# Residue outside, quarter and feature inside: another order of the first transform's data in an FFT and max-out kernel

## The chip, the cores and the metric

The kernel runs on one core of a Trainium2 chip. The metric is the device time of one execution in microseconds (us). Three runs of the kernel before the change took 436.28, 437.46 and 439.57 us: median 437.46. One further execution was profiled. Durations below are from that one.

Engines are named as the profile names them: PE is the matrix engine (TensorE), PEld its weight loads, DVE VectorE, ACT ScalarE, POOL GpSimd, SP the engine that issues most DMAs. PSUM is the memory that PE writes; SBUF holds everything else on the chip.

## The reference

A two-dimensional Fourier transform of eight batches of 3072 x 256 numbers, of which the real part is kept, and then a feed-forward layer whose hidden values are the greatest of three products:

```python
def _attn_ref(x):                       # x: (8, 3072, 256) float32
    X = np.fft.fft(x, axis=1)
    X = np.fft.fft(X, axis=2)
    return X.real.astype(np.float32)

def _moe_ref(x, w1, w2, w3, w_out):     # x: (24576, 256); w1..w3: (256, 768); w_out: (768, 256)
    h = np.maximum(np.maximum(x @ w1, x @ w2), x @ w3)
    return (h @ w_out).astype(np.float32)
```

## The kernel before, in words

The transform over 3072 rows is done as 24 x 128. **Stage one** (method `s` of class `Mix`, line 331 for the matmuls) transforms over 24 rows. Its input x0 has 96 partitions: four feature quarters g of 24 rows each; the 256 features are 4 quarters of 64 features dl. For each dl one matmul takes x0[:, dl, :] (96 x 128) as its weights and streams the 96 columns of a constant block, `m24blk`, that holds the same 24 x 24 table once for each quarter. The result is 128 x 96: 128 row positions by (quarter g, residue r), r being the 24 outputs of the short transform (13 cosines, 11 sines). Five (once four) dl share one PSUM tile, each with 96 columns side by side. `DLS` lists the 13 groups in the order in which they are done, from the middle of dl outward. ACT copies each group to `ub` in SBUF as bf16 (line 333; for batch 0 DVE takes two of them).

**The folds** (method `fold`, lines 337 to 354) use that the second transform, over the 256 features, takes features d and 256 - d together: E is their sum, O their difference. DVE computes both from `ub`, dl against 64 - dl and quarter g against 3 - g, into `zE` and `zO`, which are laid out as (dl, g, r) with r innermost: 24 residues for E and 26 for O. `fold(k, which)` does k = 0, 1, 2 from the middle outward; k = 2 also does the features 0, 64 and 128 in small instructions of their own. The instructions read and write runs of 24 residues.

**Stage two** (method `k`, lines 369 to 378, and `end`, 387 to 389) transforms over the 128 row positions. For each residue r its weights are zE[:, :, r] or zO[:, :, r], 128 partitions by 128 features. As r is innermost in zE and zO, these weights have a step of 24 or 26 elements. They multiply columns of cosine and sine tables, 128 columns for the residues 1 to 11 and 64 for 0 and 12, and one column in `end`: 53 matmuls a batch in six groups. ACT copies the results to `tE` and `tO`.

**The layer** takes tE and tO as the moving operand of further matmuls. The second transform is folded into the weights: `gE`, `gO` and `gD` are products of w2 - w1, w3 - w1 and the transform's table, `gw` is the table's product with w1 and w_out. A batch is 3 blocks of 512 row positions by 6 slices of the hidden width (18 units). In each unit `unit_plus` (lines 398, 399), `unit_minus` (406), the maxima of ACT and DVE (412, 413) and ten matmuls with w_out from a queue (422) are issued; DVE adds the linear part (451), and the result goes out by POOL's indirect DMA (456) and SP's (466). The PSUM tiles of `unit_plus`, `pse2` and `pse3`, have two buffers each.

The order of the instructions on each engine is written out by hand. While batch b goes through its 18 units, the tables `ahead0` (b = 0) and `ahead` (later batches) place the pieces of batch b + 1 behind the layer's work of single units, from unit 9, 6 or 5 on: two or three groups of stage one a unit (`s0` to `s12`), the folds (`fA0` to `fC1`, letters for k and digits for E or O), then the groups of stage two (`kE0` to `kO2`, `end`). POOL turns the input of a batch in four casts (line 118), which wait for the last fold of the batch before. For batch 0 stage one, the folds and the first groups of stage two run at the start, before any unit; there x0 keeps dl innermost, so that its weights have a step of 64 elements, while the x0 of later batches has them side by side.

Other names that the change touches: `dvec` (line 150) holds the feature numbers for the tables of the second transform, in the order of zE's 128 columns. POOL zeroes the entries of `zO` that no fold writes (lines 179, 180).

Of the kernel before, what the change touches and what calls it, by code (L numbers as in the profile page):

```python
# [10 lines left out]
BF16 = mybir.dt.bfloat16  # L11
INT32 = mybir.dt.int32
AX = mybir.ActivationFunctionType
ALU = mybir.AluOpType
# [19 lines left out]
def kernel(  # L34
# [9 lines left out]
    nc = tc.nc  # L44
# [17 lines left out]
    consts = ctx.enter_context(tc.tile_pool(name="consts", bufs=1))  # L62
# [4 lines left out]
    z_pool = ctx.enter_context(tc.tile_pool(name="zbuf", bufs=1))  # L67
    t_pool = ctx.enter_context(tc.tile_pool(name="tbuf", bufs=2))

    m24blk = consts.tile([96, 96], BF16, tag="m24blk")  # L70
# [4 lines left out]
    cos_t = consts.tile([128, 13 * 128], BF16, tag="cos_t")  # L75
    sin_t = consts.tile([128, 13 * 128], BF16, tag="sin_t")
    nsin_t = consts.tile([128, 13 * 128], BF16, tag="nsin_t")
# [11 lines left out]
    sgn = consts.tile([128, 1], FP32, tag="sgn")  # L89
    dif = consts.tile([128, 1], FP32, tag="dif")  # L90
    t_mid = consts.tile([128, 2, B], BF16, tag="t_mid")
    zO = consts.tile([128, 128 * 26], BF16, tag="zO")

    def x_rows(b):
        return x[b].rearrange("(a bb) (g dl) -> g a bb dl", bb=128, g=4)
# [32 lines left out]
    def iota(t, pattern, base=0, cm=0):  # L128
        nc.gpsimd.iota(t, pattern, base=base, channel_multiplier=cm,
                       allow_small_or_imprecise_dtypes=True)  # L130
# [17 lines left out]
    j128 = gen.tile([128, 128], FP32, tag="j128")  # L148
    iota(j128, [[24, 128]])
    dvec = gen.tile([128, 128], FP32, tag="dvec")  # L150
    for g in range(2):
        iota(dvec.rearrange("p (dl g) -> p g dl", g=2)[:, g, :], [[1, 64]], base=64 * g)

    x0_first = x0_pool.tile([96, 128 * 64], BF16, name="x0", tag="x0")
    x0v = x0_first.rearrange("p (bb dl) -> p bb dl", dl=64)
# [4 lines left out]
    for jh in range(2):  # L160
        for wsrc, wdst in ((moe_w1, w1_bf), (moe_w2, w2_bf), (moe_w3, w3_bf)):
            wld = nc.gpsimd.dma_start(
                out=wdst.rearrange("p (fc j) -> p fc j", fc=2)[:, :, jh * 384:(jh + 1) * 384],
                in_=wsrc.rearrange("(fc p) j -> p fc j", fc=2)[:, :, jh * 384:(jh + 1) * 384])
            if jh == 0 and wdst is w2_bf:
                first_half = wld
    nc.gpsimd.dma_start(out=wout_bf.rearrange("p (jc c) -> p jc c", jc=NJC),
                        in_=moe_w_out.rearrange("(jc p) c -> p jc c", jc=NJC))
# [7 lines left out]
    nc.gpsimd.tensor_scalar(out=rows_v[:, :, 11], in0=rows_v[:, :, 11], scalar1=late,  # L176
                            scalar2=None, op0=ALU.add)
    nc.gpsimd.tensor_copy(rows_m, rows_f)
    nc.gpsimd.memset(zO.rearrange("p (c r) -> p c r", r=26)[:, :, 24:26], 0.0)
    nc.gpsimd.memset(zO[:, 0:26], 0.0)  # L180

    consts_of = {}
    for (name, value) in (("half_pi", 0.5 * math.pi), ("rnd", ROUND), ("n24", -24.0),
                          ("n256", -256.0), ("n3072", -3072.0)):
        c = gen.tile([128, 1], FP32, name=name, tag=name)
# [21 lines left out]
    pi13 = gen.tile([128, 13], FP32, tag="pi13")  # L207
    nc.vector.tensor_scalar(out=pi13, in0=i13, scalar1=pidx, scalar2=None, op0=ALU.mult)
    nc.vector.tensor_tensor(
        out=m24blk.rearrange("p (g r) -> p g r", g=4),  # L210
        in0=t24.unsqueeze(1).to_broadcast([96, 4, 24]),
        in1=ind24.unsqueeze(2).to_broadcast([96, 4, 24]), op=ALU.mult)

# [2 lines left out]
    q = gen.tile([128, 13 * 128], FP32, tag="q")  # L216
    turn = float(2.0 * math.pi / 3072.0)
    for (r0, r1) in ((0, 7), (7, 13)):
        cs = slice(r0 * 128, r1 * 128)
        n = r1 - r0  # L220
        nc.vector.scalar_tensor_tensor(
            out=v[:, cs].rearrange("p (r j) -> p r j", j=128),
            in0=j128.unsqueeze(1).to_broadcast([128, n, 128]), scalar=pidx,
            in1=pi13[:, r0:r1].unsqueeze(2).to_broadcast([128, n, 128]),
# [14 lines left out]
    for fc in range(2):  # L239
# [3 lines left out]
            out=vm[:, fc * 256:(fc + 1) * 256].rearrange("p (k c) -> p k c", c=128),  # L243
            in0=dvec.unsqueeze(1).to_broadcast([128, 2, 128]), scalar=pf[:, fc:fc + 1],
            in1=half.rearrange("p (k c) -> p k c", c=128), op0=ALU.mult, op1=ALU.add)
# [15 lines left out]
    def product(i, half, jh, pool, tag):  # L261

        psg = pool.tile([128, 512], FP32, name="psg", tag=tag)
        hs = slice(half * 128, (half + 1) * 128)
        for k, (table, wt) in enumerate(((md, (w2_bf, w3_bf)[i]), (nmd, w1_bf))):
            for fc in range(2):
                nc.tensor.matmul(  # L267
                    psg[:, 0:384], table[fc][:, hs],
                    wt[:, fc * DFF + jh * 384: fc * DFF + jh * 384 + 384],
                    start=(k == 0 and fc == 0), stop=(k == 1 and fc == 1))  # L270
        return psg
# [43 lines left out]
    class Mix:  # L315

        def __init__(self, b):
            self.b = b
            self.ub = u_pool.tile([128, 64 * 96], BF16, name="ub", tag="ub")
            self.zE = z_pool.tile([128, 128 * 24], BF16, name="zE", tag="zE")  # L320
            self.tE = t_pool.tile([128, NHALF], BF16, name="tE", tag="tE")
            self.tO = t_pool.tile([128, NHALF], BF16, name="tO", tag="tO")
            self.u = self.ub.rearrange("p (dl g r) -> p dl g r", g=4, r=24)
            self.e = self.zE.rearrange("p (dl g r) -> p dl g r", g=2, r=24)
            self.o = zO.rearrange("p (dl g r) -> p dl g r", g=2, r=26)

        def s(self, k, x0, pool=ps_f, evict=nc.scalar.copy):
            (d0, d1) = DLS[k]
            ps1 = pool.tile([128, 512], FP32, name="ps1", tag="ps")
            for i in range(d1 - d0):  # L330
                nc.tensor.matmul(ps1[:, i * 96:(i + 1) * 96], x0[:, d0 + i, :], m24blk,  # L331
                                 start=True, stop=True)
            evict(out=self.ub[:, d0 * 96:d1 * 96], in_=ps1[:, 0:(d1 - d0) * 96])  # L333

        def fold(self, k, which):

            u, e, o = self.u, self.e, self.o
            dst, op = ((e, ALU.add), (o, ALU.subtract))[which]
            for (lo, hi) in (((20, 45),), ((10, 20), (45, 55)), ((1, 10), (55, 64)))[k]:
                for g in range(2):  # L340
                    nc.vector.tensor_tensor(
                        out=dst[:, lo:hi, g, 0:24], in0=u[:, lo:hi, g, :],
                        in1=u[:, 64 - lo:64 - hi:-1, 3 - g, :], op=op)
            if k < 2:
                return
            nc.vector.tensor_tensor(out=dst[:, 0, 1, 0:24], in0=u[:, 0, 1, :],
                                    in1=u[:, 0, 3, :], op=op)
            if which == 0:
                nc.vector.tensor_copy(e[:, 0, 0, :], u[:, 0, 0, :])
            else:  # L350
                nc.vector.tensor_scalar(out=o[:, 0, 0, 1:12], in0=u[:, 0, 2, 13:24],
                                        scalar1=-1.0, scalar2=None, op0=ALU.mult)
                nc.vector.tensor_copy(o[:, 0, 0, 13:24], u[:, 0, 2, 1:12])
                self.folded = nc.vector.tensor_copy(o[:, 0, 0, 24:26], u[:, 0, 2, 0:13:12])

        def k(self, which, g):

            er = self.zE.rearrange("p (c r) -> p c r", r=24)
            orr = zO.rearrange("p (c r) -> p c r", r=26)
            parts = [(r, r * 128, 128) for r in range(4 * g + 1, min(4 * g + 5, 12))]  # L360
            if g == 2:
                parts += [(0, 0, 64), (12, 12 * 128, 64)]
            ps2 = ps_f.tile([128, 512], FP32, name="ps2", tag="ps")
            c0 = 0
            for (r, k0, wd) in parts:
                outsl = ps2[:, c0:c0 + wd]
                if which == 0:
                    two = 1 <= r <= 11
                    nc.tensor.matmul(outsl, er[:, :, r], cos_t[:, k0:k0 + wd],  # L369
                                     start=True, stop=not two)  # L370
                    if two:
                        nc.tensor.matmul(outsl, er[:, :, 12 + r], sin_t[:, k0:k0 + wd],  # L372
                                         start=False, stop=True)
                else:
                    io = 24 if r == 0 else 25 if r == 12 else 12 + r
                    nc.tensor.matmul(outsl, orr[:, :, r], nsin_t[:, k0:k0 + wd],  # L376
                                     start=True, stop=False)
                    nc.tensor.matmul(outsl, orr[:, :, io], cos_t[:, k0:k0 + wd],  # L378
                                     start=False, stop=True)
                c0 += wd  # L380
            nc.scalar.copy(out=(self.tE, self.tO)[which][:, g * 512:(g + 1) * 512], in_=ps2)  # L381

        def end(self):
            er = self.zE.rearrange("p (c r) -> p c r", r=24)
            orr = zO.rearrange("p (c r) -> p c r", r=26)
            ps3 = ps_f.tile([128, 512], FP32, name="ps3", tag="ps")
            nc.tensor.matmul(ps3[:, 0:1], er[:, :, 0], cos_t[:, 64:65], start=True, stop=True)
            nc.tensor.matmul(ps3[:, 1:2], orr[:, :, 0], nsin_t[:, 64:65], start=True, stop=False)
            nc.tensor.matmul(ps3[:, 1:2], orr[:, :, 24], cos_t[:, 64:65], start=False, stop=True)
            nc.scalar.copy(out=t_mid[:, :, self.b], in_=ps3[:, 0:2])  # L390

    def unit_plus(te, to, jc, n):
# [159 lines left out]
    for k in range(13):  # L552
        m.s(k, x0f, pool=ps_s,
            evict=nc.vector.tensor_copy if k in (1, 3) else nc.scalar.copy)
# [160 lines left out]
```

## Time and profile before

| | |
|---|---|
| median of three runs | 437.46 us |
| the profiled execution | 437.27 us, of which its span 435.5 us |
| first stage-one matmul | 21.0 us after the span's start |
| TensorE's granted clock | 1.00 of full speed |
| stage one, L331 | 512 matmuls of 96 columns, 211 ns from start to end each |
| stage two, L369, L372, L376, L378, L387 to L389 | 424 matmuls of 128, 64 or 1 columns |
| folds, L341 | 160 DVE instructions on 600, 240 or 216 elements, 473, 279 and 271 ns each for O |
| evictions of stage one by ACT, L333 | 102, 556 ns each |

Times in the profile are from the start of the span. A line of instructions in order of time has the start, the time from there to the end of the last of the group, the engine, the line of the kernel, the operation with its tiles (output <- inputs), the shape and how many. In brackets stands how long the engine was idle before, and what ended that. A line of a table of groups has, behind the count, the busy time in us and the mean duration of one in ns, and then the idle time before them. PE's matmuls overlap one another: one starts while those before it still drain.

### The profile page before, as it was taken

Reading aid. Unit: us, or ns where it says so; the run is one execution under the profiler, and the core shown is the slowest. Engines: PE = TensorE matmul, PEld = TensorE weight load, DVE = VectorE, ACT = ScalarE, POOL = GpSimd, SP = SyncE. Lnnn points to the kernel's source line nnn. Section 1 sums busy time; section 2 is a strip of 40 time slices with the busy share of each in tenths; the row PEclk is TensorE's granted clock in tenths of the full one; section 3 lists DMA queues with packets and bytes.
Section 4 is the critical chain, followed back from the end, with each engine's and each line's share of the span. In section 5 each row is a group of like instructions: output and inputs, shape, how many; then the busy total and the mean of one; then the engine's idle time right before and its main releaser. Section 6 shows DMA issues by size and latency. Waiting matters only on the chain.

```text
span 435.5 us, 9209 instructions
## 1 busy us (share of the span) xinstructions
PE 413.3 (95%) x3252; PEld 277.8 (64%) x3252; DVE 309.6 (71%) x643; ACT 274.2 (63%) x512; POOL 237.8 (55%) x256
## 2 busy tenths in 40 slices
PE   0499999999999999999999999999999999999996
PEld 0275666666676667666676667666676666665665
DVE  7766668765975688666976679666976679567673
ACT  3576668667755776657765676657765676654550
POOL 7646661796269714974279514974279612214320
PEclk9999999999999999999999999999999999999999
DMA  9999999379712968169822968159822222111313
GB/s 118 121 160 129 135 169 177 103 146 169 181 53 69 162 139 189 64 115 168 165 87 76 176 123 198 61 114 165 167 92 74 73 62 75 61 50 55 105 62 132
DMA packets 127333, 51.58 MB, mean 118 GB/s; under 512 B 109233, under 2 KB 124344, under 8 KB 127288
## 3 DMA queue, kind: packets, MB, share of 16 engines
q1 hardware_dynamic: 104936, 35.80, 44.1%
q0 software_dynamic: 20624, 14.68, 17.2%
q10 hardware_dynamic: 1728, 0.52, 0.7%
q8 instruction: 25, 0.41, 0.4%
q14 instruction: 20, 0.16, 0.2%
HBM read 28.31 MB, written 25.17 MB: 123 GB/s over the span
## 4 chain that ended last, share of the span: by engine, by line
PE 90%; DVE 3%; ACT 2%; DMA 1%; POOL 1%; SPq 1%; ACTq 0%; issue 0%; POOLq 0%
PE po L422 28%; PE pse L398 14%; PE pse L406 14%; PE pse L399 14%; PE ps L331 6%; PE po L446 4%; PE pl L438 2%; PE ps L378 1%; DMA xs<-in_x_dram 1%; PE ps L369 1%; PE ps L376 1%; PE ps L372 1%; PE warm L548 1%; POOL x L118 1%; PE psg L267 1%; SPq L100 1%
## 5 line engine op out<-in xcount | busy, mean ns | idle before, releaser
L412 ACT ACTIVATE stmp<-pse 128x512 bf16<-128x512 f32 x288 | 167.8, 604 | 57.5 <-PE pse L399 52.3
L456 POOL DMA_INDIRECT out_dram<-ot,rows_m x92 | 100.2, 1089 | 166.2 <-DVE ot L451 156.2
L413 DVE TENSOR_TENSOR hp<-pse,stmp 128x512 bf16<-128x512 f32 x144 | 99.5, 691 | 100.6 <-ACT stmp L412 61.4
L118 POOL CAST x<-xs 96x2048 bf16<-96x2048 f32 x28 | 106.2, 3801 | 10.3 <-DMA xs<-in_x_dram 7.9
L398 PE MATMUL pse<-tE,gE 128*128 128x512 bf16 x288 | 109.2, 379 | 0.4
L399 PE MATMUL pse<-tO,gO 128*128 128x512 bf16 x288 | 109.0, 379 | 0.0
L413 DVE TENSOR_TENSOR hm<-pse,stmp 128x512 bf16<-128x512 f32 x144 | 98.8, 686 | 7.6 <-ACT stmp L412 7.3
L422 PE MATMUL po<-wout_bf,hp 128*128 128x256 bf16 x576 | 86.1, 273 | 0.0
L406 PE MATMUL pse<-tO,gD 128*128 128x512 bf16 x288 | 85.6, 379 | 0.0
L422 PE MATMUL po<-wout_bf,hm 128*128 128x256 bf16 x576 | 78.6, 273 | 0.0
L333 ACT CAST ub<-ps 128x480 bf16<-128x480 f32 (+1 forms) x102 | 51.7, 556 | 35.0 <-PE ps L331 35.0
L422 PEld LDWEIGHTS <-hp 128*128 128x128 bf16 x576 | 56.4, 98 | 26.1
L422 PEld LDWEIGHTS <-hm 128*128 128x128 bf16 x576 | 56.3, 98 | 16.3
L451 DVE TENSOR_TENSOR ot<-po,even 128x512 f32<-128x512 f32 x92 | 62.8, 683 | 0.0
L406 PEld LDWEIGHTS <-gD 128*128 128x128 bf16 x288 | 27.9, 98 | 32.1
L398 PEld LDWEIGHTS <-gE 128*128 128x128 bf16 x288 | 28.6, 99 | 19.5 <-issue 0.8
L399 PEld LDWEIGHTS <-gO 128*128 128x128 bf16 x288 | 28.2, 98 | 19.9 <-issue 1.6
L446 PE MATMUL po<-gw,tO 128*128 128x512 bf16 x92 | 34.9, 379 | 0.0
L331 PE MATMUL ps<-m24blk,x 96*128 96x96 bf16 x512 | 33.3, 211 | 0.9 <-POOL x L118 0.5
L331 PEld LDWEIGHTS <-x 96*128 96x128 bf16 x512 | 30.5, 111 | 3.0 <-POOL x L118 0.7
L381 ACT CAST tO<-ps 128x512 bf16<-128x512 f32 x24 | 14.0, 585 | 24.8 <-PE ps L378 24.8
L442 ACT COPY even<-pl 128x512 f32<-128x512 f32 x46 | 27.3, 594 | 0.3
(123 smaller groups left out, 335.9 us busy)
## 6 DMA issues: line engine op xcount, KB each, us to landing
xs<-in_x_dram SPq DMA_DIRECT2D x112, 192.0 KB
out_dram<-ot SPq DMA_DIRECT2D x90, 128.0 KB
out_dram<-ot,rows_m POOLq DMA_INDIRECT x92, 3.9
w_bf<-in_moe_w_dram POOLq DMA_DIRECT2D x6, 192.0 KB, 5.9
out_dram<-ot SPq DMA_DIRECT2D x17, 64.0 KB
xs<-in_x_dram SPq DMA_DIRECT2D x8, 96.0 KB
x<-in_x_dram POOLq DMA_DIRECT2D x8, 96.0 KB, 11.3
xs<-in_x_dram ACTq DMA_DIRECT2D x4, 96.0 KB
```

The costliest lines, as they stand in the source:

```text
L118: cast = nc.gpsimd.tensor_copy(turned[b][:, :, ch * 32:(ch + 1) * 32], raw.pop((b, ch)).rearrange("p (bb dl) -> p dl bb", dl=64))
L331: nc.tensor.matmul(ps1[:, i * 96:(i + 1) * 96], x0[:, d0 + i, :], m24blk, start=True, stop=True)
L333: evict(out=self.ub[:, d0 * 96:d1 * 96], in_=ps1[:, 0:(d1 - d0) * 96])
L398: nc.tensor.matmul(pse[:, 0:n], gE[i][:, js], te, start=True, stop=False)
L399: nc.tensor.matmul(pse[:, 0:n], gO[i][:, js], to, start=False, stop=True)
L406: nc.tensor.matmul(pse, gD[i][:, js], to, start=False, stop=True, skip_group_check=True)
L412: nc.scalar.activation(out=stmp[:, 0:n], in_=pses[0][:, 0:n], func=AX.Relu)
L413: nc.vector.tensor_tensor(out=dst, in0=src3, in1=stmp[:, 0:n], op=ALU.max)
L422: nc.tensor.matmul(po, hcols(jc), wout_bf[:, jc * 256:(jc + 1) * 256], start=False, stop=(jc == NJC - 1), skip_group_check=True)
L446: nc.tensor.matmul(po, to[:, cp], gw[:, 256:768], start=True, stop=True)
L451: nc.vector.tensor_tensor(out=ot.rearrange("p (h c) -> p h c", h=2), in0=po.rearrange("p (h c) -> p h c", h=2), in1=lin.unsqueeze(1).to_br ...
L456: stored(nc.gpsimd.indirect_dma_start(out, bass.IndirectOffsetOnAxis(ap=rows_m[0:128 - lo, b * 12 + slot: b * 12 + slot + 1], axis=0), ot[ ...
```

## The change

Stage one's matmul for feature dl writes its 96 columns not side by side but with a step of n words in PSUM, n being the features of the group (5, or 4 in the last), so that the n features stand innermost. The columns of `m24blk` are put in the order (residue, quarter) instead of (quarter, residue). A group in PSUM, and after ACT's copy in `ub`, is then (residue, quarter, feature of the group): rows of 20 numbers for one residue (16 in the last group).

The folds write zE and zO as (residue, position), 128 positions to a residue. Two quarters of five features make ten positions that belong together, and the folds go in runs of ten: they read the first ten numbers of a row of 20 and, backwards, the last ten of the row of the mirrored group. The first and the last group (dl 0 to 4, 60 to 63) are folded by separate instructions. A batch's fold instructions for E are 10 in place of 12, and for O 12 in place of 14. Stage two's weights are zE[:, r, :] and zO[:, r, :], 128 elements side by side. `dvec` numbers the features in the new order, and the zeroing of zO follows.

```diff
-    for g in range(2):
-        iota(dvec.rearrange("p (dl g) -> p g dl", g=2)[:, g, :], [[1, 64]], base=64 * g)
+    iota(dvec[:, 0:120], [[5, 12], [64, 2], [1, 5]])
+    iota(dvec[:, 120:128], [[64, 2], [1, 4]], base=60)
...
-    nc.gpsimd.memset(zO.rearrange("p (c r) -> p c r", r=26)[:, :, 24:26], 0.0)
-    nc.gpsimd.memset(zO[:, 0:26], 0.0)
+    zOr = zO.rearrange("p (r c) -> p r c", c=128)
+    nc.gpsimd.memset(zO[:, 24 * 128:26 * 128], 0.0)
+    nc.gpsimd.memset(zOr[:, 0:24, 0], 0.0)
...
-        out=m24blk.rearrange("p (g r) -> p g r", g=4),
+        out=m24blk.rearrange("p (r g) -> p g r", g=4),
...
+        def u(self, p0, n=1):
+
+            if p0 == 12:
+                return self.ub[:, 12 * 480:].rearrange("p (q r c) -> p q r c", q=1, r=24)
+            return self.ub[:, p0 * 480:(p0 + n) * 480].rearrange("p (q r c) -> p q r c", q=n, r=24)
...
+            n = d1 - d0
             ps1 = pool.tile([128, 512], FP32, name="ps1", tag="ps")
-            for i in range(d1 - d0):
-                nc.tensor.matmul(ps1[:, i * 96:(i + 1) * 96], x0[:, d0 + i, :], m24blk,
-                                 start=True, stop=True)
-            evict(out=self.ub[:, d0 * 96:d1 * 96], in_=ps1[:, 0:(d1 - d0) * 96])
+            ps1v = ps1[:, 0:n * 96].rearrange("p (c i) -> p i c", i=n)
+            for i in range(n):
+                nc.tensor.matmul(ps1v[:, i, :], x0[:, d0 + i, :], m24blk, start=True, stop=True)
+            evict(out=self.ub[:, d0 * 96:d1 * 96], in_=ps1[:, 0:n * 96])
...
-            u, e, o = self.u, self.e, self.o
-            dst, op = ((e, ALU.add), (o, ALU.subtract))[which]
-            for (lo, hi) in (((20, 45),), ((10, 20), (45, 55)), ((1, 10), (55, 64)))[k]:
-                for g in range(2):
-                    nc.vector.tensor_tensor(
-                        out=dst[:, lo:hi, g, 0:24], in0=u[:, lo:hi, g, :],
-                        in1=u[:, 64 - lo:64 - hi:-1, 3 - g, :], op=op)
+            z, op = ((self.zEr, ALU.add), (zOr, ALU.subtract))[which]
+
+            def dst(p0, n):
+                return z[:, 0:24, p0 * 10:(p0 + n) * 10].rearrange("p r (q c) -> p q r c", c=10)
+
+            for (p0, n) in (((4, 3), (7, 2)), ((2, 2), (9, 2)), ((1, 1), (11, 1)))[k]:
+                nc.vector.tensor_tensor(
+                    out=dst(p0, n), in0=self.u(p0, n)[:, :, :, 0:10],
+                    in1=self.u(13 - p0 - n, n)[:, ::-1, :, 19:9:-1], op=op)
...
-            nc.vector.tensor_tensor(out=dst[:, 0, 1, 0:24], in0=u[:, 0, 1, :],
-                                    in1=u[:, 0, 3, :], op=op)
+            (first, last) = (self.u(0)[:, 0], self.u(12)[:, 0])
+            nc.vector.tensor_tensor(
+                out=z[:, 0:24, 0:10].rearrange("p r (g i) -> p r g i", g=2)[:, :, :, 1:5],
+                in0=first[:, :, 0:10].rearrange("p r (g i) -> p r g i", g=2)[:, :, :, 1:5],
+                in1=last[:, :, 15:7:-1].rearrange("p r (g i) -> p r g i", g=2), op=op)
+            nc.vector.tensor_tensor(
+                out=z[:, 0:24, 120:128].rearrange("p r (g i) -> p r g i", g=2),
+                in0=last[:, :, 0:8].rearrange("p r (g i) -> p r g i", g=2),
+                in1=first[:, :, 19:9:-1].rearrange("p r (g i) -> p r g i", g=2)[:, :, :, 0:4],
+                op=op)
+            nc.vector.tensor_tensor(out=z[:, 0:24, 5], in0=first[:, :, 5], in1=first[:, :, 15],
+                                    op=op)
...
-                    nc.tensor.matmul(outsl, er[:, :, r], cos_t[:, k0:k0 + wd],
+                    nc.tensor.matmul(outsl, er[:, r, :], cos_t[:, k0:k0 + wd],
                                      start=True, stop=not two)
```

The copies of feature 128's residues (and of feature 0's) keep their counts and are written one element to a residue. The other matmuls of `k` and `end` change their weights in the same way. The order of the instructions on PE, ACT and SP is the old one.

More of the change, by code (lines that the diff above doesn't have):

```diff
@@ L91 @@
     t_mid = consts.tile([128, 2, B], BF16, tag="t_mid")
-    zO = consts.tile([128, 128 * 26], BF16, tag="zO")
+    zO = consts.tile([128, 26 * 128], BF16, tag="zO")
     def x_rows(b):
@@ L319, in __init__ @@
             self.ub = u_pool.tile([128, 64 * 96], BF16, name="ub", tag="ub")
-            self.zE = z_pool.tile([128, 128 * 24], BF16, name="zE", tag="zE")
+            self.zE = z_pool.tile([128, 24 * 128], BF16, name="zE", tag="zE")
             self.tE = t_pool.tile([128, NHALF], BF16, name="tE", tag="tE")
             self.tO = t_pool.tile([128, NHALF], BF16, name="tO", tag="tO")
-            self.u = self.ub.rearrange("p (dl g r) -> p dl g r", g=4, r=24)
-            self.e = self.zE.rearrange("p (dl g r) -> p dl g r", g=2, r=24)
@@ L325, in __init__ @@
-            self.o = zO.rearrange("p (dl g r) -> p dl g r", g=2, r=26)
+            self.zEr = self.zE.rearrange("p (r c) -> p r c", c=128)
+        def u(self, p0, n=1):
+            if p0 == 12:
+                return self.ub[:, 12 * 480:].rearrange("p (q r c) -> p q r c", q=1, r=24)
+            return self.ub[:, p0 * 480:(p0 + n) * 480].rearrange("p (q r c) -> p q r c", q=n, r=24)
         def s(self, k, x0, pool=ps_f, evict=nc.scalar.copy):
             (d0, d1) = DLS[k]
+            n = d1 - d0
@@ L348, in fold @@
+            nc.vector.tensor_tensor(out=z[:, 0:24, 5], in0=first[:, :, 5], in1=first[:, :, 15],
+                                    op=op)
             if which == 0:
-                nc.vector.tensor_copy(e[:, 0, 0, :], u[:, 0, 0, :])
+                nc.vector.tensor_copy(z[:, :, 0], first[:, :, 0])
             else:
-                nc.vector.tensor_scalar(out=o[:, 0, 0, 1:12], in0=u[:, 0, 2, 13:24],
+                nc.vector.tensor_scalar(out=z[:, 1:12, 0], in0=first[:, 13:24, 10],
                                         scalar1=-1.0, scalar2=None, op0=ALU.mult)
-                nc.vector.tensor_copy(o[:, 0, 0, 13:24], u[:, 0, 2, 1:12])
@@ L354, in fold @@
-                self.folded = nc.vector.tensor_copy(o[:, 0, 0, 24:26], u[:, 0, 2, 0:13:12])
+                nc.vector.tensor_copy(z[:, 13:24, 0], first[:, 1:12, 10])
+                self.folded = nc.vector.tensor_copy(z[:, 24:26, 0], first[:, 0:13:12, 10])
         def k(self, which, g):
-            er = self.zE.rearrange("p (c r) -> p c r", r=24)
-            orr = zO.rearrange("p (c r) -> p c r", r=26)
+            er, orr = self.zEr, zOr
             parts = [(r, r * 128, 128) for r in range(4 * g + 1, min(4 * g + 5, 12))]
@@ L368, in k @@
                     two = 1 <= r <= 11
-                    nc.tensor.matmul(outsl, er[:, :, r], cos_t[:, k0:k0 + wd],
+                    nc.tensor.matmul(outsl, er[:, r, :], cos_t[:, k0:k0 + wd],
                                      start=True, stop=not two)
                     if two:
-                        nc.tensor.matmul(outsl, er[:, :, 12 + r], sin_t[:, k0:k0 + wd],
+                        nc.tensor.matmul(outsl, er[:, 12 + r, :], sin_t[:, k0:k0 + wd],
                                          start=False, stop=True)
@@ L375, in k @@
                     io = 24 if r == 0 else 25 if r == 12 else 12 + r
-                    nc.tensor.matmul(outsl, orr[:, :, r], nsin_t[:, k0:k0 + wd],
+                    nc.tensor.matmul(outsl, orr[:, r, :], nsin_t[:, k0:k0 + wd],
                                      start=True, stop=False)
-                    nc.tensor.matmul(outsl, orr[:, :, io], cos_t[:, k0:k0 + wd],
+                    nc.tensor.matmul(outsl, orr[:, io, :], cos_t[:, k0:k0 + wd],
                                      start=False, stop=True)
@@ L383, in end @@
         def end(self):
-            er = self.zE.rearrange("p (c r) -> p c r", r=24)
-            orr = zO.rearrange("p (c r) -> p c r", r=26)
+            er, orr = self.zEr, zOr
             ps3 = ps_f.tile([128, 512], FP32, name="ps3", tag="ps")
-            nc.tensor.matmul(ps3[:, 0:1], er[:, :, 0], cos_t[:, 64:65], start=True, stop=True)
-            nc.tensor.matmul(ps3[:, 1:2], orr[:, :, 0], nsin_t[:, 64:65], start=True, stop=False)
-            nc.tensor.matmul(ps3[:, 1:2], orr[:, :, 24], cos_t[:, 64:65], start=False, stop=True)
+            nc.tensor.matmul(ps3[:, 0:1], er[:, 0, :], cos_t[:, 64:65], start=True, stop=True)
+            nc.tensor.matmul(ps3[:, 1:2], orr[:, 0, :], nsin_t[:, 64:65], start=True, stop=False)
+            nc.tensor.matmul(ps3[:, 1:2], orr[:, 24, :], cos_t[:, 64:65], start=False, stop=True)
             nc.scalar.copy(out=t_mid[:, :, self.b], in_=ps3[:, 0:2])
```

## The prediction

> **What bounds the kernel now.** I read the page's busy line and chain of waits first, then PE and DVE instructions in order of time, then DVE by windows.
>
> ```profile
> span 435.5 us, 9209 instructions
> PE 413.3 (95%) x3252; PEld 277.8 (64%) x3252; DVE 309.6 (71%) x643; ACT 274.2 (63%) x512; POOL 237.8 (55%) x256
> PE 90%; DVE 3%; ACT 2%; DMA 1%; POOL 1%; SPq 1%; ACTq 0%; issue 0%; POOLq 0%
> ```
>
> PE holds 90% of the chain that ended last, and between the first stage-one matmul (21.0 us) and the last store it hardly stops. So a matmul that takes a longer or a shorter place in PE's stream moves the end by just that much. The place is the distance from its start to the next start, not its duration, since matmuls overlap. PE in order of time, at three places (start, duration to the last end, group):
>
> ```profile
> 100.42 0.82 PE L422 MATMUL po<-wout_bf,hp 128*128 128x256 bf16 x6
> 101.08 0.59 PE L331 MATMUL ps<-m24blk,x 96*128 96x96 bf16 x10
> 101.51 0.38 PE L398 MATMUL pse<-tE,gE 128*128 128x512 bf16 x1
> 101.73 0.38 PE L399 MATMUL pse<-tO,gO 128*128 128x512 bf16 x1
> ...
> 135.44 0.23 PE L378 MATMUL ps<-cos_t,zO 128*128 128x128 bf16 x1
> 135.50 0.20 PE L376 MATMUL ps<-nsin_t,zO 128*128 128x64 bf16 x1
> ...
> 135.75 0.21 PE L387 MATMUL ps<-cos_t,zE 128*128 128x1 bf16 x1
> 135.81 0.20 PE L388 MATMUL ps<-nsin_t,zO 128*128 128x1 bf16 x1
> 135.88 0.20 PE L389 MATMUL ps<-cos_t,zO 128*128 128x1 bf16 x1
> 135.94 0.38 PE L398 MATMUL pse<-tE,gE 128*128 128x512 bf16 x1
> ```
>
> A 512-column matmul takes 101.73 - 101.51 = 0.216 us, a 256-column one (101.08 - 100.42) / 6 = 0.109 us: 0.416 ns for a column and 2.9 ns beside it. By that line 96 columns cost 43 ns, and ten stage-one matmuls do take (101.51 - 101.08) / 10 = 43 ns. Stage two is off the line: from 135.44 on, 128, 64 and one column all take 60 to 70 ns. What doesn't depend on columns isn't the stream of columns; it is the weight load in front of each matmul:
>
> ```profile
> L446 PEld LDWEIGHTS <-tO 128*128 128x128 bf16 x92 | 9.0, 98 | 1.0
> L369 PEld LDWEIGHTS <-zE 128*128 128x128 bf16 x104 | 14.7, 160 | 1.1 <-DVE zE L349 0.8
> ```
>
> Unit-step weights load in 98 ns, those of stage two (steps of 24 and 26 elements) in 160.
>
> **Stage two: the saving.** The batch mixed from 122.91 us on has its 53 stage-two matmuls in six runs of 0.54, 0.52, 0.56, 0.52, 0.52 and 0.83 us, 3.49 in all. With unit-step weights I put them on the line: 44 matmuls of 128 columns at 56 ns and nine of 64 or 1 column at 43 ns, the shortest place that unit-step weights show here (stage one): 2.46 + 0.39 = 2.85 us. Saved: 0.64 us a batch, eight batches **-5.1 us**. The nine could go lower, by 0.1 us a batch; above nothing there is no loss, since the loads get shorter.
>
> **Stage one: the price.** 448 matmuls of the batches 1 to 7 now write their 96 columns five words apart instead of side by side. Every matmul of this profile writes PSUM with unit step, so the price isn't shown. The near rows are stepped operands of PE itself. Stage one of batch 0 does the same matmul with weights 64 elements apart:
>
> ```profile
> 21.00 3.30 PE L331 MATMUL ps<-m24blk,x 96*128 96x96 bf16 x35
> 24.13 0.49 PE L267 MATMUL psg<-w_bf,md_all 128*128 128x384 bf16 x2
> ```
>
> (24.13 - 21.00) / 35 = 89 ns against 43, a factor of two; stage two's step of 24 gives 67 against at most 43, a factor of 1.6. So the place of 43 ns goes to between 43 (nothing; a gain has no reason here, the stream being on its line) and 89. I take the streaming part twice, near the upper row, because that is the same instruction on the same engine: 2 x 40 + 2.9 = 83 ns, **+40 ns x 448 = +17.9 us**. The factor 1.6 gives +24 ns, 10.8 us. In batch 0 the place of 89 ns is set by the weights and covers an 83 ns write; without that cover its 64 matmuls cost 2.6 us more.
>
> [...]
>
> **The folds.** ScalarE's evictions keep their shapes and stay contiguous on both sides: nothing. A batch's fold instructions go from 12 + 14 to 10 + 12, with the same 3024 elements for each of E and O, but in runs of 10 rather than 24, written 128 apart, with the second input read backwards inside a run. DVE at the start, where the folds are alone:
>
> ```profile
> 24.06 0.85 DVE L341 TENSOR_TENSOR zE<-ub 128x600 bf16<-128x600 bf16 x2 [0.39 <-ACT ub L333]
> 24.83 0.85 DVE L341 TENSOR_TENSOR zO<-ub 128x600 bf16<-128x600 bf16 x2
> 26.44 0.86 DVE L341 TENSOR_TENSOR zE<-ub 128x240 bf16<-128x240 bf16 x4 [0.76 <-ACT ub L333]
> 27.22 0.86 DVE L341 TENSOR_TENSOR zO<-ub 128x240 bf16<-128x240 bf16 x4
> ```
>
> 600 elements take 0.77 / 2 = 385 ns, 240 take 0.78 / 4 = 195: 68 ns and 0.528 ns an element. The lower price: E becomes 720 (448 ns), three of 480 (321 each), two of 240 (195), two of 192 (169), two of 24 (83 as now), 2.31 us, against 770 + 780 + 728 + 166 = 2.44 before: -0.14 us, -0.3 a batch with O, hidden under PE. The upper price: one element at a time, as the fp32 row L26 has it (896 elements 1092 ns, 768 elements 957: 1.055 ns an element), +0.53 ns x 6048 = +3.2 us a batch. I take the lower, zero on the path, because the stepped rows that the folds already read show no price over it; nothing reads backwards inside a bf16 run, so the upper end stays a rival. Its cover:
>
> ```profile
> 110.00:123.45 13.45, 13.45 (x112) 9.05 (x110) 12.76 (x33) 9.22 (x18) 4.18 (x8) 1.00 0.61 152
> ```
>
> Through the stretch of the folds DVE is busy 12.76 of 13.45 us: 0.69 us are free.
>
> The index ramp for the second DFT, the zeroing of zO and the weight block of stage one are reordered in the first 5 us with the same counts, at 0.1 to 0.35 us each; POOL's two ramps stay ahead of the same loads. Nothing for them. PE, ACT and SP issue in the old order, no DMA moves, no wait is added.
>
> **Sum:** -5.1 + 17.9 + 0 = +12.8 us on the profiled execution's 437.27 (span 435.5 and 1.8 around it; 0.2 under the median of 437.46): **450 us**. This case alone runs from 437.3 - 5.1 + 10.8 = 443 to 437.3 - 5.1 + 89's 46 ns x 448 (20.6) + 2.6 = 455.
>
> **Rivals.**
> - *The stepped PSUM write is free* (the other side). [...] Then only the saving is left: 437.3 - 5.1 = **432**. It decides at 5.1 us / 448 = 11 ns: if stage one takes less than 54 ns, the change wins. Chance 0.27; since the gain, 1.2%, lies on the 1% that a measurement of this kernel can tell from no change, 0.20 of it counts as faster, 0.07 as the same.
> - *A write price of some 11 ns*, the break-even: **437**. Chance 0.06.
> - *Folds one element at a time, write free.* Of 3.2 us a batch, DVE's free 0.69 us takes part, and the PSUM pair another 0.4: hm read till 115.59 (114.91 + 0.68), and PE writes that second tile again from 115.97. The other 2.1 us stop PE, in seven batches 14.7; at the start, where PE waits for the last E and O folds as it is (0.40 and 0.43 us), DVE's two gaps of 0.76 and 0.68 us take up 1.4 of 3.2 and the rest, 1.8, is late: 437.3 - 5.1 + 14.7 + 1.8 = **449**. Chance 0.08. [...]
> - *Both prices*: stage one's stretch, 0.4 us in each of some 3.5 units that hold folds, gives DVE 1.4 us more cover, so 0.7 of the 2.1 us is left: 450 + 0.7 x 7 + 1.8 = **457**. Chance 0.12.
> - *A write price of much over twice*: at three times the stream, 17.9 us more: **468**. Chance 0.05.
> - *Stage two doesn't speed up*: spoken against by the one-column matmuls at 66 ns; its chance is in the widths.
>
> The forecast keeps 0.42. Slower by over 1%: 0.42 + 0.08 + 0.12 + 0.05 = 0.67; within: 0.07 + 0.06 = 0.13; faster: 0.20. The range reaches from 431.5 (write free, the nine short matmuls lower) to 456 and leaves out 0.17.
>
> **What will show it.** Stage one: ten matmuls L331 from start to next start, 0.83 us against 0.43. Stage two: eight in 0.45 against 0.54, weight loads at 98 ns. Folds: 720 elements near 0.53 us (the 0.45 from start to start and what an end lies behind) if the price is the lower, near 0.9 if the upper, and then PE waits for DVE in the fold stretch. Wrong it would be first of all by a stage-one place that stays at 43 ns.

## The result and the profile after

The changed kernel takes 448.61 us in the median of six runs (448.39 to 451.21), the kernel before 438.61 us (six runs, 436.28 to 439.57): the ratio of their means is 1.0251, with a 95% interval from 1.0215 to 1.0287. The forecast was 450 us. The profiled execution took 448.53 us, 11.3 more than the 437.27 of before; its span grew by 11.2. By the medians it is 10.0: the six runs of the kernel before have a median 1.2 us above that of the three known at the forecast.

From the page of the changed kernel, the span, the busy line and the chain by engine:

```profile
span 446.7 us, 9177 instructions
PE 424.3 (95%) x3252; PEld 288.5 (65%) x3252; DVE 308.7 (69%) x611; ACT 276.0 (62%) x512; POOL 237.7 (53%) x256
PE 93%; DMA 3%; DVE 2%; ACT 1%; issue 0%; ACTq 0%; DVEq 0%
```

PE is still the bound, with as many instructions as before and 11.0 us more of busy time. DVE has 32 instructions fewer and 0.9 us less to do. So the time is looked for in PE's stream alone, again from start to start. PE in order of time, changed kernel (L338 is stage one, L414 and L415 are `unit_plus`, L393, L395 and L403 to L405 stage two):

```profile
101.74 0.99 PE L338 MATMUL ps<-m24blk,x 96*128 96x96 bf16 x10
102.53 0.42 PE L414 MATMUL pse<-tE,gE 128*128 128x512 bf16 x1
102.78 0.38 PE L415 MATMUL pse<-tO,gO 128*128 128x512 bf16 x1
...
138.11 0.22 PE L395 MATMUL ps<-cos_t,zO 128*128 128x128 bf16 x1
138.17 0.19 PE L393 MATMUL ps<-nsin_t,zO 128*128 128x64 bf16 x1
138.20 0.19 PE L395 MATMUL ps<-cos_t,zO 128*128 128x64 bf16 x1
...
138.28 0.17 PE L403 MATMUL ps<-cos_t,zE 128*128 128x1 bf16 x1
138.31 0.16 PE L404 MATMUL ps<-nsin_t,zO 128*128 128x1 bf16 x1
138.34 0.16 PE L405 MATMUL ps<-cos_t,zO 128*128 128x1 bf16 x1
138.36 0.38 PE L414 MATMUL pse<-tE,gE 128*128 128x512 bf16 x1
```

Ten stage-one matmuls take 102.53 - 101.74 = 0.79 us, where they took 0.43. The 512-column matmul right behind them takes 0.25 us in place of 0.216: 0.04 us more belong to the group. That is 0.40 us for ten, 40 ns for each. Stage two has gone the other way: 128 columns take 0.06 us (138.17 - 138.11; eight of them 0.45, 56 ns each), 64 columns 0.03, one column 0.02 to 0.03, where nearly all had taken 60 to 70 ns (some of 64 columns 40). The weight loads of stage two in the table of groups:

```profile
L386 PEld LDWEIGHTS <-zE 128*128 128x128 bf16 x104 | 9.8, 98 | 0.8 <-DVE zE L367 0.5
```

98 ns in place of 160, as L446's loads with unit step had before. With the places of all matmuls of the two traces added up, from start to start, by line:

| | before, us | after, us | difference |
|---|---|---|---|
| stage one, 512 matmuls | 25.36 | 41.19 | +15.8 |
| `unit_plus`, first line (behind stage one) | 62.52 | 64.28 | +1.8 |
| stage two, 424 matmuls | 28.95 | 22.86 | -6.1 |
| products with w_out, with the waits behind them | 127.48 | 126.86 | -0.6 |
| all matmuls, first to last start | 415.42 | 426.65 | +11.2 |

The lines that the table leaves out add 0.3. The -0.6 is a wait that was there before and is no longer: in the profiled execution of before, stage one of batch 1 waited for POOL's last cast of its input. The idle time was 0.47 us; with it the w_out matmul in front had a place of 0.74 us, where 0.11 is usual. Kernel before, PE in order of time:

```profile
58.30 0.60 PE L331 MATMUL ps<-m24blk,x 96*128 96x96 bf16 x10 [0.47 <-POOL x L118]
```

In the changed kernel's profiled execution that group starts at 57.39 us with no wait, since the cast was done at 52.72 + 3.72 = 56.44, before PE came. POOL in order of time, changed kernel; the bracket shows that the cast itself waits for its load:

```profile
52.72 3.72 POOL L118 CAST x<-xs 96x2048 bf16<-96x2048 f32 x1 [1.73 <-DMA xs<-in_x_dram]
```

The folds cost PE nothing: in the changed kernel it waits for none of them from batch 1 on, and at the start 0.60 us for O, where it waited 0.40 us for E and 0.43 for O before. Groups of the changed kernel:

```profile
L349 DVE TENSOR_TENSOR zE<-ub 128x480 bf16<-128x480 bf16 x24 | 9.0, 404 | 0.8 <-ACT ub L339 0.8
L349 DVE TENSOR_TENSOR zE<-ub 128x720 bf16<-128x720 bf16 x8 | 4.2, 525 | 0.4 <-ACT ub L339 0.4
...
L349 DVE TENSOR_TENSOR zE<-ub 128x240 bf16<-128x240 bf16 x16 | 3.8, 277 | 0.2 <-ACT ub L339 0.2
```

From 240 to 720 elements the duration grows from 277 to 525 ns: 0.517 ns an element, about the rate of before (0.528), in runs of ten with one input read backwards.

### The profile page after: what moved, and what is told of

Read it like the earlier page. It is cut to its first block, busy times and chain, and to the rows that moved or that the text cites. A ratio compares the mean times of both kernels' runs of the same rounds, so it can differ in the third digit from the quotient of the medians.

```text
span 446.7 us, 9177 instructions
## 1 busy us (share of the span) xinstructions
PE 424.3 (95%) x3252; PEld 288.5 (65%) x3252; DVE 308.7 (69%) x611; ACT 276.0 (62%) x512; POOL 237.7 (53%) x256
## 4 chain that ended last, share of the span: by engine, by line
PE 93%; DMA 3%; DVE 2%; ACT 1%; issue 0%; ACTq 0%; DVEq 0%
PE po L438 28%; PE pse L414 14%; PE pse L422 14%; PE pse L415 14%; PE ps L338 9%; PE po L462 4%; DMA xs<-in_x_dram 3%; PE pl L454 2%; PE ps L393 1%; PE ps L395 1%; PE ps L386 1%; PE ps L389 1%; PE psg L268 1%; DVE hm L429 0%; ACT ub L339 0%; PE pst L298 0%
## 5 line engine op out<-in xcount | busy, mean ns | idle before, releaser
L428 ACT ACTIVATE stmp<-pse 128x512 bf16<-128x512 f32 x288 | 170.8, 602 | 57.5 <-PE pse L415 52.4
L472 POOL DMA_INDIRECT out_dram<-ot,rows_m x92 | 101.9, 1107 | 179.1 <-DVE ot L467 172.0
L414 PE MATMUL pse<-tE,gE 128*128 128x512 bf16 x288 | 111.1, 386 | 0.4
L415 PE MATMUL pse<-tO,gO 128*128 128x512 bf16 x288 | 109.2, 379 | 0.0
L118 POOL CAST x<-xs 96x2048 bf16<-96x2048 f32 x28 | 104.4, 3739 | 8.7 <-DMA xs<-in_x_dram 6.3
L338 PE MATMUL ps<-m24blk,x 96*128 96x96 bf16 x512 | 51.4, 283 | 1.2 <-DVE dif L255 0.9
L338 PEld LDWEIGHTS <-x 96*128 96x128 bf16 x512 | 44.6, 139 | 3.0 <-DVE dif L255 1.4
L415 PEld LDWEIGHTS <-gO 128*128 128x128 bf16 x288 | 30.0, 104 | 20.0 <-issue 1.8
L414 PEld LDWEIGHTS <-gE 128*128 128x128 bf16 x288 | 30.0, 104 | 19.4 <-issue 0.8
## 6 DMA issues: line engine op xcount, KB each, us to landing
x<-in_x_dram POOLq DMA_DIRECT2D x8, 96.0 KB, 11.3
```

The source lines that it names most:

```text
L118: cast = nc.gpsimd.tensor_copy(turned[b][:, :, ch * 32:(ch + 1) * 32], raw.pop((b, ch)).rearrange("p (bb dl) -> p dl bb", dl=64))
L338: nc.tensor.matmul(ps1v[:, i, :], x0[:, d0 + i, :], m24blk, start=True, stop=True)
L414: nc.tensor.matmul(pse[:, 0:n], gE[i][:, js], te, start=True, stop=False)
L415: nc.tensor.matmul(pse[:, 0:n], gO[i][:, js], to, start=False, stop=True)
L428: nc.scalar.activation(out=stmp[:, 0:n], in_=pses[0][:, 0:n], func=AX.Relu)
L472: stored(nc.gpsimd.indirect_dma_start(out, bass.IndirectOffsetOnAxis(ap=rows_m[0:128 - lo, b * 12 + slot: b * 12 + slot + 1], axis=0), ot[ ...
```

## The experiments

The theory, an estimate from 79 ns a matmul (and 4 behind it) in place of 43: a written column that stands alone takes as long as two that stand side by side; that is the whole loss, and stage two's saving is real beside it. The rivals: the folds have a share in the loss; every jump in the written pattern costs, however the columns are grouped; the price hangs on the distance of the jumps; any two neighbours will do, wherever they start. The time of the kernel before is the median of nine runs here (for e5 of seven), and the ratios are of means.

**e1: the stepped write alone, in the kernel before.**

```diff
-            for i in range(d1 - d0):
-                nc.tensor.matmul(ps1[:, i * 96:(i + 1) * 96], x0[:, d0 + i, :], m24blk,
+            n = d1 - d0
+            ps1v = ps1[:, 0:n * 96].rearrange("p (c i) -> p i c", i=n)
+            for i in range(n):
+                nc.tensor.matmul(ps1v[:, i, :], x0[:, d0 + i, :], m24blk,
```

> The kernel before, with one thing added: stage one writes its 96 columns five words apart. The columns of the groups are then in another order than the folds read them, so the sums are of other numbers; counts and shapes are those of before. If the stepped PSUM write is the whole loss: ten stage-one matmuls take 0.79 us and the matmul behind them 0.04 more, +0.40 us for ten, 448 of them: +17.9 us, 455 to 456 us, with stage two at 67 ns a matmul as before. If part of the loss of the changed kernel is the folds' (runs of ten, read backwards): less, 450 or below, since the folds are those of before.

Measured: 455.47 us against 437.75, ratio 1.0394 (1.0367 to 1.0422). PE in order of time:

```profile
104.14 0.99 PE L333 MATMUL ps<-m24blk,x 96*128 96x96 bf16 x10
104.92 0.42 PE L400 MATMUL pse<-tE,gE 128*128 128x512 bf16 x1
105.18 0.38 PE L401 MATMUL pse<-tO,gO 128*128 128x512 bf16 x1
```

0.78 us for ten and 0.26 for the matmul behind them, as in the changed kernel, with folds and stage two of before. 455.47 - 437.75 = 17.7 us, against 17.9 expected: the stepped write alone costs as much as the whole loss. A share of the folds would have to hide in the 2 us over which the runs of before spread, and e2 and e3, which keep the new folds, come to 432 us without it.

**e2: the same order of the data, written in pairs.** In the changed kernel, the two quarters of a half (g = 0, 1 or 2, 3) are put innermost, so that two of a matmul's columns stand side by side; a row of `ub` is then (half, feature, quarter of the half), and the folds' runs of ten read backwards just as before. The small folds of the first and last group, and `dvec`, follow (of these, the new lines alone are shown):

```diff
-    iota(dvec[:, 0:120], [[5, 12], [64, 2], [1, 5]])
-    iota(dvec[:, 120:128], [[64, 2], [1, 4]], base=60)
+    iota(dvec[:, 0:120], [[5, 12], [1, 5], [64, 2]])
+    iota(dvec[:, 120:128], [[1, 4], [64, 2]], base=60)
...
-            ps1v = ps1[:, 0:n * 96].rearrange("p (c i) -> p i c", i=n)
+            ps1v = ps1[:, 0:0 + n * 96].rearrange("p (h i two) -> p i h two", i=n, two=2)
...
-                nc.tensor.matmul(ps1v[:, i, :], x0[:, d0 + i, :], m24blk, start=True, stop=True)
-            evict(out=self.ub[:, d0 * 96:d1 * 96], in_=ps1[:, 0:n * 96])
+                nc.tensor.matmul(ps1v[:, i], x0[:, d0 + i, :], m24blk, start=True, stop=True)
+            evict(out=self.ub[:, d0 * 96:d1 * 96], in_=ps1[:, 0:0 + n * 96])
...
+            nc.vector.tensor_tensor(out=z[:, 0:24, 2:10], in0=first[:, :, 2:10],
+                                    in1=last[:, :, 15:7:-1], op=op)
+            nc.vector.tensor_tensor(out=z[:, 0:24, 120:128], in0=last[:, :, 0:8],
+                                    in1=first[:, :, 19:11:-1], op=op)
+            nc.vector.tensor_tensor(out=z[:, 0:24, 1], in0=first[:, :, 1], in1=first[:, :, 11],
+                                    op=op)
```

> The changed kernel, with stage one's columns written in pairs: (residue, half, feature, quarter of the half), so that two columns stand side by side and the next pair follows ten words on; folds, stage two and tables follow. If PSUM takes two neighbouring words at a time, the pairs cost nothing: ten stage-one matmuls 0.43 us, only stage two's saving is left, the span some 5.5 us under before: 432 to 433 us, ratio 0.987. If every jump costs, there are half as many: +20 ns a matmul, 441 us. If any pattern that isn't contiguous costs the same: 448.6 as in the changed kernel.

Measured: 431.99 us against 437.75, ratio 0.986 (0.9834 to 0.9886): 1.4% under the kernel before, and under the changed one. PE in order of time:

```profile
101.16 0.59 PE L338 MATMUL ps<-m24blk,x 96*128 96x96 bf16 x10
101.58 0.38 PE L409 MATMUL pse<-tE,gE 128*128 128x512 bf16 x1
101.80 0.38 PE L410 MATMUL pse<-tO,gO 128*128 128x512 bf16 x1
```

0.42 us for ten and 0.22 behind them: 48 pairs, each ten words behind the one before, cost what 96 columns side by side cost. So it is not the jump that has a price.

**e3: a contiguous write, and the eviction turns the data.** In the changed kernel:

```diff
-            ps1v = ps1[:, 0:n * 96].rearrange("p (c i) -> p i c", i=n)
...
-                nc.tensor.matmul(ps1v[:, i, :], x0[:, d0 + i, :], m24blk, start=True, stop=True)
-            evict(out=self.ub[:, d0 * 96:d1 * 96], in_=ps1[:, 0:n * 96])
+                nc.tensor.matmul(ps1[:, i * 96:(i + 1) * 96], x0[:, d0 + i, :], m24blk,
+                                 start=True, stop=True)
+            evict(out=self.ub[:, d0 * 96:d1 * 96].rearrange("p (c i) -> p c i", i=n),
+                  in_=ps1[:, 0:n * 96].rearrange("p (i c) -> p c i", i=n))
```

> The changed kernel, with stage one's columns written side by side and the eviction reading them 96 words apart, so that ub, folds and stage two are those of the changed kernel. If only PE's write has a price: evictions stay at 0.56 us each, 432 to 433 us, ratio 0.987. If an eviction reading with a step takes twice its time (1.1 us for 480 columns), ACT gets 0.9 us more in units where it was busy 2.0 of 2.8 us, and PE waits for the two PSUM tiles: 440 us or more.

Measured: 432.45 us, ratio 0.9861 (0.9834 to 0.9887), the same as e2. PE in order of time:

```profile
100.87 0.59 PE L337 MATMUL ps<-m24blk,x 96*128 96x96 bf16 x10
101.30 0.38 PE L415 MATMUL pse<-tE,gE 128*128 128x512 bf16 x1
```

Ten matmuls take 0.43 us again. The evictions in the table of groups, here reading 96 words apart, and of e2, reading side by side:

```profile
L339 ACT CAST ub<-ps 128x480 bf16<-128x480 f32 x94 | 48.8, 562 | 34.5 <-PE ps L337 33.9 <-issue 0.7
```

```profile
L339 ACT CAST ub<-ps 128x480 bf16<-128x480 f32 x94 | 48.8, 562 | 35.9 <-PE ps L338 34.2 <-issue 1.1 <-PE pse L410 0.5
```

562 ns both ways: ACT reads PSUM with this step at no price. Of the two, only PE's write has one.

**e4: the distance.** In the changed kernel, two features are interleaved word by word, and the fifth stands by itself; the folds then read other numbers:

```diff
-            ps1v = ps1[:, 0:n * 96].rearrange("p (c i) -> p i c", i=n)
...
-                nc.tensor.matmul(ps1v[:, i, :], x0[:, d0 + i, :], m24blk, start=True, stop=True)
+                o = (i // 2) * 192
+                dst = ps1[:, o + i % 2:o + 192:2] if i < 4 else ps1[:, 384:480]
+                nc.tensor.matmul(dst, x0[:, d0 + i, :], m24blk, start=True, stop=True)
```

> The changed kernel, with stage one's columns written two words apart for four features of five (two features interleaved) and side by side for the fifth; the numbers that the folds read are then others, counts and shapes stay. If every column that doesn't follow its neighbour costs the same: four of five matmuls at 79 ns, (4 x 79 + 43) / 5 = 72 ns a matmul, 445 us. If the price grows with the distance of two words: less, 50 to 60 ns, 436 to 440 us.

Measured, in one run: 445.43 us. PE in order of time:

```profile
101.47 0.91 PE L339 MATMUL ps<-m24blk,x 96*128 96x96 bf16 x10
102.22 0.38 PE L415 MATMUL pse<-tE,gE 128*128 128x512 bf16 x1
```

0.75 us for ten, of which the two side by side take 0.086: 83 ns for each of the eight with a step of two words, as much as with a step of five (79 + 4). Between two words and five the distance has no part in it.

**e5: the same pairs, one word further on.** In e2:

```diff
-            ps1v = ps1[:, 0:0 + n * 96].rearrange("p (h i two) -> p i h two", i=n, two=2)
+            ps1v = ps1[:, 1:1 + n * 96].rearrange("p (h i two) -> p i h two", i=n, two=2)
-            evict(out=self.ub[:, d0 * 96:d1 * 96], in_=ps1[:, 0:0 + n * 96])
+            evict(out=self.ub[:, d0 * 96:d1 * 96], in_=ps1[:, 1:1 + n * 96])
```

> The kernel of e2 with stage one's PSUM group moved on by one word, so that each pair starts at an odd word; the eviction reads it from there, and the results stay the same. If PSUM takes two neighbouring words wherever they start: 432 us as in e2. If it takes an aligned pair of words at a time, each pair is split again: ten stage-one matmuls take 0.79 us, +17.9 us on e2, 449 to 450 us.

Measured: 449.02 us against 437.68, ratio 1.0247 (1.0219 to 1.0276): 17.0 us lost on e2 by one word of offset. PE in order of time:

```profile
102.08 0.99 PE L338 MATMUL ps<-m24blk,x 96*128 96x96 bf16 x10
102.86 0.42 PE L409 MATMUL pse<-tE,gE 128*128 128x512 bf16 x1
103.12 0.38 PE L410 MATMUL pse<-tO,gO 128*128 128x512 bf16 x1
```

0.78 and 0.26 us again. So not any two neighbours will do: the pairs are free where each starts at an even word of the tile (0.42 us for ten, e2), and cost as much as single columns where each starts at an odd one. A row of columns side by side that starts at an odd word was not run, so it is not shown whether an odd start costs without pairs too; the single columns of the changed kernel, which start at odd and even words in turn, take 80 to 83 ns either way behind the first of a group (medians by the place in the group).

## Why the prediction was right

*What bounds the kernel.* Right: PE's stream set the time before and after, and the differences of its places from start to start add up to the 11.2 us of the span.

*Stage one.* Forecast +17.9 us at 40 ns a matmul, by twice the streaming part; measured 40 ns, +17.6 in the trace (15.8 and the 1.8 behind the groups), and 17.7 by e1 alone. The range of 24 to 46 ns came from weights with a step, the nearest rows there were. That the like held for written columns was a guess when it was made: those rows show weight loads, and that their factor of two is also that of the write is luck. e1, e2, e4 and e5 show when the price falls due; neither the distance (two or five words) nor a jump as such (ten words, between pairs) sets it: ten matmuls take 0.42 us where the columns stand in pairs that start at even words (e2), and 0.78 us where each column stands alone (e1) or each pair starts at an odd word (e5); alone at two words apart (e4) a matmul takes the same 83 ns as at five. How PSUM takes the columns is not shown beyond these times.

*The cover in batch 0.* Right. There the place is set by the weights with a step of 64. Changed kernel, PE in order of time:

```profile
21.39 3.35 PE L338 MATMUL ps<-m24blk,x 96*128 96x96 bf16 x35 [0.93 <-DVE dif L255]
24.54 0.53 PE L268 MATMUL psg<-w_bf,md_all 128*128 128x384 bf16 x2
```

(24.54 - 21.39) / 35 = 90 ns, against 89 before.

*Stage two.* The mechanism was right, the size too small: forecast -5.1 us, measured -6.1. The term that was mis-sized is that of the nine short matmuls of a batch, put at 43 ns, with 0.1 us a batch left open below. They take 20 to 30 ns, 0.14 us a batch less. A batch's six runs now take 0.45, 0.44, 0.45, 0.45, 0.39 and 0.53 us, 2.71 in place of the 2.85 forecast; before it was 3.49.

*The folds.* Right that they stay at the lower price and off the path: 0.517 ns an element, and 720 elements in 525 ns, where 0.53 us was named. Only those of 192 elements, of the first and last group, were put a little low, at 169 ns from start to start. DVE in order of time, changed kernel and then e2, where L355 has 192 elements too:

```profile
29.32 0.35 DVE L355 TENSOR_TENSOR zE<-ub 128x192 bf16<-128x192 bf16 x1 [0.37 <-ACT ub L339]
29.52 0.27 DVE L359 TENSOR_TENSOR zE<-ub 128x192 bf16<-128x192 bf16 x1
```

```profile
28.84 0.27 DVE L355 TENSOR_TENSOR zE<-ub 128x192 bf16<-128x192 bf16 x1 [0.37 <-ACT ub L339]
29.01 0.25 DVE L357 TENSOR_TENSOR zE<-ub 128x192 bf16<-128x192 bf16 x1
```

The changed kernel's L355, in runs of four of which every second starts at an odd element, takes 0.20 us to the next start, e2's, in runs of eight from even elements, 0.17. One element at a time it would be 68 + 192 x 1.055 = 271 ns, by the prediction's prices. So the rivals with folds at one element at a time are out.

*The rest of the difference.* Forecast +12.8, measured +11.3: 0.3 less in stage one, 1.0 more saved in stage two, 0.6 from the wait for POOL's cast that didn't occur, and 0.4 back at the start of stage one (PE waited 0.93 us for DVE's `dif` there, in e2 0.33). That cast was in none of the steps, and it goes the other way as well. The profiled execution of e2, PE in order of time:

```profile
59.14 0.60 PE L338 MATMUL ps<-m24blk,x 96*128 96x96 bf16 x10 [2.12 <-POOL x L118]
```

There PE came to batch 1 earlier, and waited 2.12 us, so that the span is 4.4 us under that of before (431.1 against 435.5), not 6. The cast in turn waited for its load, whose time differs between the profiles of these kernels (that last cast starts between 51.4 and 55.4 us). How much of it is due to the kernel was not tried.

*The rival on the other side*, a free write at 432 us, needed a stage-one matmul of less than 54 ns. It had 83. Its time is that of e2 and e3, which take the price away: 431.99 and 432.45 us.

## What to carry to other kernels

In a stream that PE bounds, cost a matmul by the distance to the next start, and look whether it follows the columns or the weights: stage two's matmuls took 60 to 70 ns for 1 and for 128 columns alike while their weight loads took 155 to 178 ns, and 20 to 30 and 56 ns with loads of 98. When a matmul's output is to be put in another order, try pairs of fp32 columns that start at even words (e2, 431.99 us), or write it side by side and let the eviction do the turning (e3, 432.45 us); both were free here, where single columns cost 17.7 us. Before a reordering is given up because one side of it is dear, see which other step can do it.

## What the runs showed of the hardware

- PE's PSUM write with single columns ran at about half the rate: 96 columns in 83 ns in place of 43, alike at steps of two and of five words. Pairs ten words apart that start at even words ran at the full rate (ten matmuls in 0.42 us, e2), pairs that start at odd words at half (0.78 us, e5).
- ACT's reading of 480 PSUM words, 96 words apart (e3), takes 562 ns, as long as side by side (562 ns, e2).
- Weight loads of 98 ns with unit step follow one another at less than 30 ns (one-column matmuls: three in 138.36 - 138.28 = 0.08 us); those of the same three before, with steps of 24 and 26 elements and 173 to 178 ns each, at 60 to 70 ns. The duration of these loads doesn't tell their place.
- DVE reads an input backwards in runs of ten bf16 at about the rate of 24-element forward runs: 0.517 against 0.528 ns an element. These runs start at an odd element, 19, and go down from there. An odd start on the way up is in L355 of the changed kernel, which reads and writes from element 1: 0.20 us to the next start, where the 1.055 ns an element of the fp32 row L26 would make it 0.27 (68 + 192 x 1.055 ns). So an odd start didn't bring the whole instruction down to that rate. Whether the 0.03 us over e2's L355 come from the start or from the shorter runs was not tried.
